# Decode attention on one core: score groups of one key block, a row maximum in halves, and engine programs without a block

## The chip, the cores and the metric

The kernel runs on one core of a Trainium2 chip. A core has five engines that run their own instruction streams and meet at semaphores: TensorE (PE, matmuls and the weight loads ahead of them), VectorE (DVE), ScalarE (ACT), GpSimd (POOL) and SyncE (SP), which here only issues DMAs. The metric is the device time of one execution in microseconds (us). Before the change the median of three executions is 445.27 us (445.12 to 446.51).

## The reference

One decode step of a transformer layer for 8 sequences, one token each:

```
mod = silu(c) @ w_mod                      # 1024 -> six vectors sa, ca, ga, sb, cb, gb
h   = layernorm(x) * (1 + ca) + sa
q   = h @ wq                               # 32 heads of 128
scores = q . k_cache * 128**-0.5           # 4 key/value heads, 8192 keys, each shared by 8 query heads
o   = softmax(scores) @ v_cache
x   = x + ga * (o @ wo)
h   = layernorm(x) * (1 + cb) + sb
x   = x + gb * ((relu(h @ W_gate) * (h @ W_up)) @ W_down)
```

All tensors are bf16. The key and value caches are 8 x 4 x 8192 x 128, 67 MB each; with the weights some 186 MB are read, each byte once.

## The kernel before

The kernel is written as a list of operations (`P.op`), each with its engine, the ranges it reads and the ranges it writes. `Prog` derives the waits from these ranges; each engine runs its own operations in the order in which they stand in the list. There is no scheduler behind it: the list's order is the program's order.

All large inputs come through one ring in SBUF, `arena`, on SP's queue. They are loaded in a fixed order: w_mod in two parts, wq in two, then K and V of each step m = 0 to 15 (4 MB each), wo in two, gate and up in two each, and W_down (wd) in five parts of falling size. `pump` puts the next load into the list as soon as every reader of the range it overwrites stands there; at run time the load waits for that reader. In the loop the ring has room for K and V of two steps, so K of step m+2 is issued when the last transpose of K of step m is done, and V of step m+2 when PV of step m is done.

A step m takes two of the 32 (sequence, key head) pairs, both on the 128 partitions. The keys of a step are eight blocks (`QE` = 2048 bf16 per partition). Its stages:

- `kt_part` (L428, DVE): one block is transposed in 32x32 squares into one of four buffers of `kt`. A block's buffer is free again when the scores that read it are done.
- `qk_part` (L441, PE): the scores of two blocks, i and 4+i, 8 matmuls with 512 columns. There are four stationary operands (`t`, `r`), slices of the padded queries `qpad`; each is used for the first block (h = 0) and at once for the second (h = 1). The scores of h = 0 and h = 1 lie in two neighbouring PSUM banks, and each bank is accumulated over the four groups i.
- `rowmax` (L449, DVE): one maximum over both banks, 1024 wide, negated.
- `spread` (L453, PE) and `headmax` (L458 and L461, DVE): the maximum over the rows that belong to one query.
- `expo` (L467, ACT): the exponential, with the row sums.
- `p_turn` (L474, DVE): P transposed, 64 partitions at a time.
- `pv` (L483, PE): 32 matmuls with V, in two column halves.
- `fold` (L493, L496, DVE) and `fold_pe` (L501, PE): PV's result of step m-1 is gathered; these stand among the operations of step m.

PE's order in a step is: four score groups, spread, fold_pe of the step before, PV. DVE's order is: eight transposes, two folds, row maximum, a fold, headmax, a fold, p_turn. So DVE can turn four blocks of step m+1 while PE runs PV of step m, and then waits until the first score group has freed buffers. `make_qpad` (L421, POOL) writes the queries two steps ahead.

At the end `P.emit` writes each engine's operations into a body of `nc.Block`. Each engine branches from the main block to its body, and leaves it through a barrier of all engines.

Of the kernel before, what the change touches and what calls it, by code (L numbers as in the profile page):

```python
# [7 lines left out]
ALU = mybir.AluOpType  # L8
AX = mybir.AxisListType
# [123 lines left out]
def bass_adaLN_cond__gqa_block_cached__glu_gated_reglu__decode_kernel(nc, A_x, A_k_cache, A_v_cache, A_wq, A_wo, B_x, B_W_gate, B_W_up, B_W_down, c, w_mod, out):  # L133
    B, _, D = A_x.shape
    _, G, Sk, Dh = A_k_cache.shape
# [11 lines left out]
    NKT = 4  # L147
# [4 lines left out]
    P = Prog()  # L152
    with ExitStack() as es:
        E = es.enter_context

        def sb(name, shape, dtype):
            return E(nc.sbuf_tensor(name, shape, dtype))
# [5 lines left out]
        ktb = sb("kt", [128, NKT * 2048], dt.bfloat16)  # L163
# [21 lines left out]
        qpad = sb("qpad", [128, 2, 4, 152], dt.bfloat16)  # L185
        prb = sb("prb", [128, 1024], dt.bfloat16)
        pT = sb("pT", [128, 2, 32, 2, 32], dt.bfloat16)
        negm = sb("negm", [128, 4], dt.float32)
# [14 lines left out]
        ps = E(nc.psum_tensor("ps", [128, 8, 512], dt.float32))  # L203

        sems = {("eng", e): E(nc.semaphore("s_" + e)) for e in P.ENGINES}
# [3 lines left out]
        def R(t, lo=0, hi=1):  # L209
            return (t, lo, hi)  # L210

        def bank(b, n=1):
            return ("ps", b, b + n)

        def slot_r(lo, hi):
            return ("arena", lo, hi)
# [3 lines left out]
        stream, place, cursor = [], {}, [0]  # L220
# [51 lines left out]
        def aff(e, t, base, pat):  # L272
# [7 lines left out]
             reads=[R("identf"), R("rsel")], writes=[R("rsel")])  # L280
# [8 lines left out]
                                     start=True, stop=True), reads=[R("rsel"), R("cx", 0, 2)], writes=[bank(6)])  # L289
# [4 lines left out]
             reads=[R("lt")], writes=[R("lt")])  # L294
        P.op("dve", lambda e: e.reciprocal(lu[:], lt[:]), reads=[R("lt")], writes=[R("lu")])
        P.op("dve", lambda e: e.tensor_tensor(out=hb[:], in0=lu[:], in1=c_r, op=ALU.mult),
             reads=[R("lu"), R("x_r")], writes=[R("hb")])

        def to_T(eng="dve"):
# [5 lines left out]
             reads=[R("identf")], writes=[R("dsel")])  # L305
        P.op("dve", lambda e: e.tensor_reduce(jm[:], identf[:].rearrange("p (g m j) -> p g j m", g=2, j=J), AX.X, ALU.add),
             reads=[R("identf")], writes=[R("jm")])
# [3 lines left out]
             reads=[R("identf")], writes=[R("im")])  # L311
        P.op("dve", lambda e: e.tensor_scalar(out=sel[:].rearrange("p (q r) -> p q r", q=4),
                                              in0=dsel[:, None, :].to_broadcast([128, 4, 32]), scalar1=1.0 / D, scalar2=None,
                                              op0=ALU.mult), reads=[R("dsel")], writes=[R("sel")])
        P.op("dve", lambda e: e.tensor_scalar(out=jms[:], in0=jm[:].rearrange("p g j -> p (g j)"), scalar1=scale, scalar2=None, op0=ALU.mult),
             reads=[R("jm")], writes=[R("jms")])
# [29 lines left out]
        for i in range(2):  # L346
            fns = []
            for kk in range(4 * i, 4 * i + 4):
                w = arena[:, place["wm", i] + (kk % 4) * 6 * D:place["wm", i] + (kk % 4 + 1) * 6 * D].rearrange("p (s j n) -> p s j n", s=6, j=4)
                for pr in range(3):  # L350
                    for j in range(4):
                        fns.append(lambda e, w=w, pr=pr, j=j, kk=kk: e.matmul(  # L352
                            ps[32 * j:32 * j + 32, pr, :], hT[:, kk, :], w[:, 2 * pr:2 * pr + 2, j, :],
                            start=(kk == 0), stop=(kk == KC - 1), tile_position=(0, 32 * j)))
            P.op("pe", fns, reads=[R("hT"), slot_r(place["wm", i], place["wm", i] + 24 * D)], writes=[bank(0, 3)])
        for pr in range(3):
# [3 lines left out]
                 reads=[bank(pr)], writes=[R("mod", 2 * pr, 2 * pr + 2)])  # L360
# [8 lines left out]
        for i in range(2):  # L369
            fns = []  # L370
            for kk in range(4 * i, 4 * i + 4):
                w = arena[:, place["wq", i] + (kk % 4) * 4096:place["wq", i] + (kk % 4 + 1) * 4096].rearrange("p (g z n) -> p g z n", g=4, z=2)
                for z in range(2):
                    for g in range(4):
                        fns.append(lambda e, w=w, z=z, g=g, kk=kk: e.matmul(  # L375
                            ps[32 * g:32 * g + 32, 3 + z, :], hT[:, kk, :], w[:, g, z, :],
                            start=(kk == 0), stop=(kk == KC - 1), tile_position=(0, 32 * g)))
            P.op("pe", fns, reads=[R("hT"), slot_r(place["wq", i], place["wq", i] + 2 * SLOT)], writes=[bank(3, 2)])
        qrep = ktb[:, 0:4096].rearrange("p (u q x) -> p u q x", u=4 * J, q=4)
        for z in range(2):  # L380
# [5 lines left out]
            else:  # L386
# [3 lines left out]
                 reads=[res], writes=[res])  # L390
# [3 lines left out]
        for jh in range(2):  # L394
            fns = []
# [5 lines left out]
            for t in range(2):  # L401
                for r in range(2):
# [3 lines left out]
                    if jh == 0:  # L406
                        P.op("dve", lambda e, s=src, d=dst: e.tensor_copy(d, s), reads=[bank(5 + jh)],
                             writes=[R("qR", u * 2 + jh, u * 2 + jh + 1)])
                    else:
                        P.op("act", lambda e, s=src, d=dst: e.activation(d, s, ACT.Copy), reads=[bank(5 + jh)],  # L410
                             writes=[R("qR", u * 2 + jh, u * 2 + jh + 1)])
# [3 lines left out]
        QE = SLOT // 4  # L415

        def make_qpad(m):
            if m >= M:
                return
            for Q in range(4):  # L420
                P.op("pool", lambda e, n=2 * m + Q // 2, Q=Q: e.tensor_copy(  # L421
                    qpad[32 * Q:32 * Q + 32, m % 2, :, 24 + 32 * Q:32 + 32 * Q], qR[32 * Q:32 * Q + 32, :, n, :]),
                     reads=[R("qR", 0, 8)], writes=[R("qpad", m % 2, m % 2 + 1)])

        def kt_part(m, i, h):
            lo = place["k", m] + (4 * h + i) * QE
            to = (8 * m + 2 * i + h) % NKT * QE
            P.op("dve", lambda e: e.transpose(ktb[:, to:to + QE].bitcast(dt.uint32), arena[:, lo:lo + QE].bitcast(dt.uint32)),  # L428
                 reads=[slot_r(lo, lo + QE)], writes=[R("kt", to, to + QE)])

        def qk_part(m, i):
            fns, rd = [], [R("qpad", m % 2, m % 2 + 1)]
            for h in range(2):
                to = (8 * m + 2 * i + h) % NKT * QE
                rd.append(R("kt", to, to + QE))
            for t in range(2):
                for r in range(2):
                    for h in range(2):
                        to = (8 * m + 2 * i + h) % NKT * QE
                        kv = ktb[:, to:to + QE].rearrange("p (c t k r) -> p c t k r", t=2, k=32, r=2)  # L440
                        fns.append(lambda e, t=t, r=r, h=h, kv=kv: e.matmul(  # L441
                            ps[:, 2 * (m % 2) + h, :].rearrange("p (c k) -> p c k", k=32),
                            qpad[:, m % 2, t * 2 + r, 24 - 8 * i:152 - 8 * i], kv[:, :, t, :, r],
                            start=(i == 0 and t == 0 and r == 0), stop=(i == 3 and t == 1 and r == 1)))
            P.op("pe", fns, reads=rd, writes=[bank(2 * (m % 2), 2)])

        def rowmax(m):
            b = 2 * (m % 2)
            P.op("dve", lambda e: e.tensor_reduce(negm[:, 2:3], ps[:, b:b + 2, :].rearrange("p h n -> p (h n)"), AX.X, ALU.max,  # L449
                                                  negate=True), reads=[bank(b, 2)], writes=[R("negm", 2, 3)])  # L450

        def spread(m):
            P.op("pe", lambda e: e.matmul(ps[:, 4, 0:128], negm[:, 2:3].to_broadcast([128, 128]), identf[:],  # L453
                                         start=True, stop=True), reads=[R("negm", 2, 3), R("identf")], writes=[bank(4)])

# [9 lines left out]
        def expo(m):  # L465
            z = m % 2
            P.op("act", lambda e: e.activation(prb[:], ps[:, 2 * z:2 * z + 2, :].rearrange("p h n -> p (h n)"), ACT.Exp,  # L467
                                               bias=bias[:, z:z + 1], scale=scale, accum_out=lall[:, m:m + 1]),
                 reads=[bank(2 * z, 2), R("bias", z, z + 1)], writes=[R("prb"), R("lall", m, m + 1)])
# [42 lines left out]
        make_qpad(0)  # L512
        make_qpad(1)
        for m in range(M):
            for i in range(4):
                kt_part(m, i, 0)
                kt_part(m, i, 1)
                qk_part(m, i)
            make_qpad(m + 2)
            fold(m - 1, 0)  # L520
            fold(m - 1, 1)
            rowmax(m)
            spread(m)
            fold(m - 1, 2)
            headmax(m)
            expo(m)
            fold(m - 1, 3)
            if m >= 1:
                fold_pe(m - 1)
            if m == M - 1:  # L530
                norm()
            p_turn(m)
            pv(m)
        lr = lx[:].rearrange("p n j -> p (n j)")
        P.op("dve", lambda e: e.reciprocal(lr, ps[:, 7, 0:N * J]), reads=[bank(7)], writes=[R("lx")])
        for i in range(4):
# [5 lines left out]
                                              in0=ps[:, 6, 0:N * J].rearrange("p (b h) -> p h b", b=B),  # L542
                                              in1=lr.rearrange("p (b h) -> p h b", b=B), op=ALU.mult),
             reads=[bank(6), R("lx"), R("oT")], writes=[R("oT")])


        for z in range(2):
            fns = []
            for jj in range(4):
                for g in range(G):  # L550
                    fns.append(lambda e, z=z, jj=jj, g=g: e.matmul(
                        ps[32 * g:32 * g + 32, z, 128 * jj:128 * jj + 128], oT[:, J * g + 4 * z + jj, :], identb[:],
                        start=True, stop=True, tile_position=(0, 32 * g)))
# [4 lines left out]
            else:  # L558
                P.op("act", lambda e, dst=dst, z=z: e.activation(dst, ps[:, z, :], ACT.Copy), reads=[bank(z)],
                     writes=[("kt", 512 * z, 512 * z + 512)])  # L560
        P.op("dve", lambda e: e.transpose(oX, orow.rearrange("p j d -> p (j d)").rearrange("p (x k) -> p k x", k=KO)),  # L561
             reads=[("kt", 0, 1024)], writes=[r_oX])


        for i, (r0, r1) in enumerate(wo_parts):
            lo, hi = place["wo", i], place["wo", i] + (r1 - r0) * D
            w = arena[:, lo:hi].rearrange("p (r j n) -> p r j n", r=r1 - r0, j=4)
            fns = []
            for k in range(r0, r1):
# [6 lines left out]
             reads=[bank(5), R("mod", 2, 3)], writes=[R("lu")])  # L576
        P.op("dve", lambda e: e.tensor_tensor(out=x1[:], in0=lu[:], in1=x_r, op=ALU.add),
             reads=[R("lu"), R("x_r")], writes=[R("x1")])
# [5 lines left out]
        for i, (r0, r1) in enumerate(gu_parts):  # L584
            for nm, b0 in (("gate", 0), ("up", 2)):
                lo, hi = place[nm, i], place[nm, i] + (r1 - r0) * F
                w = arena[:, lo:hi].rearrange("p (r j h n) -> p r j h n", r=r1 - r0, j=4, h=2)
                fns = []
                for kk in range(r0, r1):
                    for h in range(2):  # L590
                        for j in range(4):
                            fns.append(lambda e, w=w, r=kk - r0, kk=kk, h=h, j=j, b0=b0: e.matmul(  # L592
                                ps[32 * j:32 * j + 32, b0 + h, 0:H], hT[:, kk, :], w[:, r, j, h, :],
                                start=(kk == 0), stop=(kk == KC - 1), tile_position=(0, 32 * j)))
                P.op("pe", fns, reads=[R("hT"), slot_r(lo, hi)], writes=[bank(b0, 2)])
        for h in range(2):
            P.op("act", lambda e, h=h: e.activation(grel[:, H * h:H * h + H], ps[:, h, 0:H], ACT.Relu), reads=[bank(h)],
                 writes=[("kt", 4096 + FJ * h, 4096 + FJ * h + FJ)])
            P.op("dve", lambda e, h=h: e.tensor_tensor(out=hrow[:, H * h:H * h + H], in0=ps[:, 2 + h, 0:H],  # L599
                                                       in1=grel[:, H * h:H * h + H], op=ALU.mult),  # L600
                 reads=[bank(2 + h), ("kt", 4096 + FJ * h, 4096 + FJ * h + FJ)], writes=[("kt", 2048 + H * h, 2048 + H * h + H)])
        P.op("dve", lambda e: e.transpose(hmT, hrow.rearrange("p (x k) -> p k x", k=KF)), reads=[("kt", 2048, 2048 + FJ)],
             writes=[r_hmT])
        for i, (r0, r1) in enumerate(wd_parts):
            lo, hi = place["wd", i], place["wd", i] + (r1 - r0) * D
            w = arena[:, lo:hi].rearrange("p (r j n) -> p r j n", r=r1 - r0, j=4)
            fns = []
            for k in range(r0, r1):
# [6 lines left out]
             reads=[bank(4), R("mod", 5, 6)], writes=[R("lu")])  # L615
        P.op("dve", lambda e: e.tensor_tensor(out=ob[:], in0=lu[:], in1=x1[:], op=ALU.add),
             reads=[R("lu"), R("x1")], writes=[R("ob")])
        o2 = out.rearrange("b o d -> (b o) d")
        for j in range(4):
            P.op("sp" if j % 2 == 0 else "act",  # L620
                 lambda e, j=j: e.dma_start(o2[:, 256 * j:256 * (j + 1)], ob[32 * j:32 * j + B, :]),
                 reads=[R("ob")], writes=[("out", j, j + 1)], dma=True)
        P.op("sp", [], reads=[("out", 0, 4)])

        P.plan()
        block = E(nc.Block())
        bass_engs = {"sp": nc.sync, "act": nc.scalar, "pool": nc.gpsimd, "dve": nc.vector, "pe": nc.tensor}
        starters = {"sp": block.sync, "act": block.scalar, "pool": block.gpsimd, "dve": block.vector, "pe": block.tensor}
        for name in P.ENGINES:
            def body(_, name=name):  # L630
                P.emit(name, bass_engs[name], sems)
            starters[name](body)


# [26 lines left out]
```

## Time and profile before

| | before |
|---|---|
| median of 3 executions | 445.27 us |
| the profiled execution, its own time | 446.51 us |
| its span, first to last instruction | 444.7 us |
| mean granted TensorE clock | 0.812 |
| DMA queue of SP | 185.64 MB, 97.7% of 16 engines' span |
| key transposes (L428) | 128 of 1213 ns, 148.0 us |
| score matmuls (L441) | 512, 121.5 us busy |
| PV matmuls (L483) | 512, 91.9 us busy |
| row maximum (L449) | 16 of 1225 ns, 19.6 us |
| spread (L453) | 32 matmul records, 7.8 us |

The profile is of one execution. Busy times of engines overlap, so they don't add up to the span. A matmul's busy time counts from its start to its end through the array, and matmuls follow each other more closely than that. The chain of waits is followed back from the last instruction: what released each piece of work. "us to landing" of a DMA counts from its issue on SP to its completion, the time in the queue included. In a table by stretches of time each row has busy time and number of instructions of PE, PE's weight loads, DVE, ACT and POOL, then the granted clock of TensorE (1.00 is full), the busy share of the DMA engines and GB/s.

### The profile page before, as it was taken

To read this page: it belongs to the slowest core of one execution; us is meant where nothing else is said; L and a number is where in the kernel's file an instruction comes from. 1 tells how busy PE (TensorE), PEld (TensorE's weight loads), DVE (VectorE), ACT (ScalarE), POOL (GpSimd) and SP (SyncE) were. 2 spreads that over 40 slices of the span, in tenths; PEclk is the share of its full clock that TensorE was granted. 3 is DMA by queue.
4 is the path that set the end of the run, shared out by engine and by line. 5 is a ranking of instruction groups with operands and counts; after the bars stand their busy time and mean duration, and the time that the engine had idled before them with its cause. 6 is when DMAs were issued, how large, how long until landed. Compare 5 with 4: busy or idle time off the path is not lost.

```text
span 444.7 us, 3991 instructions
## 1 busy us (share of the span) xinstructions
PE 269.2 (61%) x1691; PEld 121.4 (27%) x1691; DVE 258.9 (58%) x340; ACT 28.8 (6%) x48; POOL 19.8 (4%) x77
## 2 busy tenths in 40 slices
PE   0062427667484949576775849495857668556635
PEld 0021112323132323223232314232322323235312
DVE  0233056667777776857667777767576677753120
ACT  1100011110101010101001010101010010110100
POOL 6000010000000000000000000000000000000000
PEclk9997568696978879696969788797969697876775
DMA  8999999999999999999999999999999999999993
GB/s 354 427 445 426 424 433 454 424 430 426 424 451 433 432 424 427 438 439 430 433 424 427 439 439 429 430 404 424 405 433 385 419 398 406 412 438 424 435 415 158
DMA packets 6946, 185.90 MB, mean 418 GB/s; under 512 B 816, under 2 KB 912, under 8 KB 1168
## 3 DMA queue, kind: packets, MB, share of 16 engines
q1 hardware_dynamic: 6896, 185.64, 97.7%
q8 instruction: 13, 0.21, 0.2%
q14 instruction: 5, 0.04, 0.0%
q10 hardware_dynamic: 32, 0.01, 0.0%
HBM read 185.63 MB, written 0.02 MB: 417 GB/s over the span
## 4 chain that ended last, share of the span: by engine, by line
PE 40%; DVE 35%; DMA 18%; ACT 5%; issue 2%; SPq 0%
PE ps L483 21%; DVE kt L428 17%; PE ps L441 14%; DVE pT L474 9%; DMA arena<-in_w_mod_dram 7%; DMA arena<-in_A_k_cache_dram 6%; DMA arena<-in_B_W_down_dram 5%; DVE negm L449 4%; ACT prb L467 4%; PE ps L453 2%; PE ps L571 1%; DVE mj L458 1%; PE ps L592 1%; DVE mjt L461 1%; PE ps L352 1%
## 5 line engine op out<-in xcount | busy, mean ns | idle before, releaser
L428 DVE STREAM_TRANSPOSE kt<-arena 128x1024 uint32<-128x1024 uint32 x128 | 148.0, 1213 | 52.4 <-PE ps L441 47.6
L441 PE MATMUL ps<-kt,qpad 128*128 128x512 bf16 x512 | 121.5, 383 | 23.2 <-DVE kt L428 23.2
L483 PE MATMUL ps<-arena,pT 128*64 128x512 bf16 x512 | 91.9, 537 | 50.8 <-DVE pT L474 50.8
L441 PEld LDWEIGHTS ps<-kt,qpad 128*128 128x128 bf16 x512 | 45.6, 97 | 97.5 <-DVE kt L428 32.5
L483 PEld LDWEIGHTS ps<-arena,pT 128*64 128x64 bf16 x512 | 43.9, 152 | 93.4 <-issue 87.6
L474 DVE STREAM_TRANSPOSE pT<-prb 64x1024 bf16<-64x1024 bf16 x32 | 39.6, 1239 | 15.9 <-ACT prb L467 15.4
L467 ACT ACTIVATE prb<-ps,bias 128x1024 bf16<-128x1024 f32 x16 | 17.8, 1113 | 290.6 <-DVE mjt L461 290.6
L449 DVE TENSOR_REDUCE negm<-ps 128x1 f32<-128x1024 f32 x16 | 19.6, 1225 | 22.8 <-PE ps L441 22.8
L421 POOL COPY qpad<-qR 32x32 bf16<-32x32 bf16 x64 | 13.0, 203 | 322.5 <-PE ps L441 268.5
L453 PE MATMUL ps<-identf,negm 128*128 128x128 f32 x32 | 7.8, 325 | 21.2 <-DVE negm L449 21.2
L496 DVE SCALAR_TENSOR_TENSOR om<-ps,im,om 128x128 f32<-128x128 f32 x48 | 16.6, 346 | 0.6
L375 PE MATMUL ps<-arena,hT 128*32 128x512 bf16 x64 | 6.8, 602 | 14.1 <-DMA arena<-in_A_wq_dram 14.1
L501 PE MATMUL ps<-jmp,om 128*128 128x16 f32 x32 | 6.3, 272 | 14.7 <-DVE om L496 14.7
L592 PE MATMUL ps<-arena,hT 128*32 128x448 bf16 x128 | 9.3, 464 | 5.9 <-DMA arena<-in_B_W_up_dram 3.5
L453 PEld LDWEIGHTS ps<-identf,negm 128*128 128x128 f32 x32 | 4.7, 186 | 29.1 <-DVE negm L449 27.2
L290 DVE CAST cxr<-ps 128x512 bf16<-128x512 f32 x1 | 0.7, 691 | 19.1 <-PE ps L288 19.1
L288 PE MATMUL ps<-cx,rsel 32*128 32x512 bf16 x1 | 0.6, 582 | 18.5 <-DMA cx<-in_A_x_dram 18.5
L610 PE MATMUL ps<-arena,kt 128*32 128x256 bf16 x112 | 6.9, 415 | 7.5 <-DMA arena<-in_B_W_down_dram 7.5
L385 DVE CAST kt<-ps 128x512 bf16<-128x512 f32 x1 | 0.7, 691 | 17.4 <-PE ps L375 17.4
L501 PEld LDWEIGHTS ps<-jmp,om 128*128 128x128 f32 x32 | 4.8, 188 | 18.0 <-DVE om L496 16.9
L599 DVE TENSOR_TENSOR kt<-ps,kt 128x448 bf16<-128x448 f32 x2 | 1.2, 620 | 13.1 <-PE ps L592 13.1
L571 PE MATMUL ps<-arena,kt 128*32 128x256 bf16 x128 | 6.5, 398 | 2.7 <-DVE kt L561 2.7
(79 smaller groups left out, 93.1 us busy)
## 6 DMA issues: line engine op xcount, KB each, us to landing
arena<-in_A_k_cache_dram SPq DMA_DIRECT2D x16, 4096.0 KB, 22.5
arena<-in_A_v_cache_dram SPq DMA_DIRECT2D x16, 4096.0 KB, 18.1
arena<-in_w_mod_dram SPq DMA_DIRECT2D x2, 6144.0 KB, 17.3
arena<-in_A_wq_dram SPq DMA_DIRECT2D x2, 4096.0 KB, 20.6
arena<-in_A_wo_dram SPq DMA_DIRECT2D x2, 4096.0 KB, 16.0
arena<-in_B_W_gate_dram SPq DMA_DIRECT2D x2, 3584.0 KB, 18.6
arena<-in_B_W_up_dram SPq DMA_DIRECT2D x2, 3584.0 KB, 22.5
arena<-in_B_W_down_dram SPq DMA_DIRECT2D x1, 3584.0 KB, 24.5
```

What stands on the lines that cost most here:

```text
L421: P.op("pool", lambda e, n=2 * m + Q // 2, Q=Q: e.tensor_copy(qpad[32 * Q:32 * Q + 32, m % 2, :, 24 + 32 * Q:32 + 32 * Q], qR[32 * Q:32 * ...
L428: P.op("dve", lambda e: e.transpose(ktb[:, to:to + QE].bitcast(dt.uint32), arena[:, lo:lo + QE].bitcast(dt.uint32)), reads=[slot_r(lo, lo ...
L441: fns.append(lambda e, t=t, r=r, h=h, kv=kv: e.matmul(ps[:, 2 * (m % 2) + h, :].rearrange("p (c k) -> p c k", k=32), qpad[:, m % 2, t * 2 ...
L449: P.op("dve", lambda e: e.tensor_reduce(negm[:, 2:3], ps[:, b:b + 2, :].rearrange("p h n -> p (h n)"), AX.X, ALU.max, negate=True), reads= ...
L453: P.op("pe", lambda e: e.matmul(ps[:, 4, 0:128], negm[:, 2:3].to_broadcast([128, 128]), identf[:], start=True, stop=True), reads=[R("negm" ...
L467: P.op("act", lambda e: e.activation(prb[:], ps[:, 2 * z:2 * z + 2, :].rearrange("p h n -> p (h n)"), ACT.Exp, bias=bias[:, z:z + 1], scal ...
L474: P.op("dve", lambda e, g=g: e.transpose(pT[64 * g:64 * g + 64, z, :, g, :], prb[64 * g:64 * g + 64, :]), reads=[R("prb"), R("pT", z, z + ...
L483: fns.append(lambda e, t=t: e.matmul(ps[64 * (t % 2):64 * (t % 2) + 64, 5, :].rearrange("p (i d) -> p i d", d=Dh), pT[:, z, t].rearrange(" ...
L496: P.op("dve", lambda e, i=i: e.scalar_tensor_tensor(out=om[:], in0=ps[:, 5, Dh * i:Dh * i + Dh], scalar=im[:, i:i + 1], in1=om[:], op0=ALU ...
L501: P.op("pe", lambda e: e.matmul(ps[:, 6, 16 * m:16 * m + 16], om[:], jmp[:].rearrange("p g j -> p (g j)"), start=True, stop=True), reads=[ ...
L571: fns.append(lambda e, w=w, r=k - r0, k=k, j=j: e.matmul(ps[32 * j:32 * j + 32, 5, 0:256], oX[:, k, :], w[:, r, j, :], start=(k == 0), sto ...
L592: fns.append(lambda e, w=w, r=kk - r0, kk=kk, h=h, j=j, b0=b0: e.matmul(ps[32 * j:32 * j + 32, b0 + h, 0:H], hT[:, kk, :], w[:, r, j, h, : ...
```

## The change

There are three edits.

1. Scores. `qk_part` takes one key block in place of two: 4 matmuls a group and eight groups a step, each right behind its own transpose. The blocks are taken in memory order, so groups 0 to 3 fill the first PSUM bank and groups 4 to 7 the second. A stationary operand is used for one matmul and then changed.
2. Row maximum. `rowmax` is called for each bank: 512 wide, for the first bank behind the sixth transpose and score group, for the second where the whole one stood. `spread` begins with the minimum of the two negated values, one element per partition, on DVE.
3. Program. The operations are written into the main block, without `nc.Block`: no branch at the start and no barrier of all engines at the end.

```diff
-        def kt_part(m, i, h):
-            lo = place["k", m] + (4 * h + i) * QE
-            to = (8 * m + 2 * i + h) % NKT * QE
+        def kt_part(m, e8):
+            lo = place["k", m] + e8 * QE
+            to = (8 * m + e8) % NKT * QE
...
-        def qk_part(m, i):
-            fns, rd = [], [R("qpad", m % 2, m % 2 + 1)]
-            for h in range(2):
-                to = (8 * m + 2 * i + h) % NKT * QE
-                rd.append(R("kt", to, to + QE))
+        def qk_part(m, e8):
+            to = (8 * m + e8) % NKT * QE
+            i = e8 % 4
+            b = 2 * (m % 2) + e8 // 4
+            kv = ktb[:, to:to + QE].rearrange("p (c t k r) -> p c t k r", t=2, k=32, r=2)
+            fns = []
             for t in range(2):
                 for r in range(2):
-                    for h in range(2):
...
-        def rowmax(m):
-            b = 2 * (m % 2)
-            P.op("dve", lambda e: e.tensor_reduce(negm[:, 2:3], ps[:, b:b + 2, :].rearrange("p h n -> p (h n)"), AX.X, ALU.max,
-                                                  negate=True), reads=[bank(b, 2)], writes=[R("negm", 2, 3)])
+        def rowmax(m, h):
+            b = 2 * (m % 2) + h
+            P.op("dve", lambda e: e.tensor_reduce(negm[:, h:h + 1], ps[:, b, :], AX.X, ALU.max, negate=True),
+                 reads=[bank(b)], writes=[R("negm", h, h + 1)])
 
         def spread(m):
+            P.op("dve", lambda e: e.tensor_tensor(out=negm[:, 2:3], in0=negm[:, 0:1], in1=negm[:, 1:2], op=ALU.min),
+                 reads=[R("negm", 0, 2)], writes=[R("negm", 2, 3)])
...
-            for i in range(4):
-                kt_part(m, i, 0)
-                kt_part(m, i, 1)
-                qk_part(m, i)
+            for e8 in range(8):
+                kt_part(m, e8)
+                qk_part(m, e8)
+                if e8 == 5:
+                    rowmax(m, 0)
             make_qpad(m + 2)
             fold(m - 1, 0)
             fold(m - 1, 1)
-            rowmax(m)
+            rowmax(m, 1)
             spread(m)
...
-        block = E(nc.Block())
...
-        for name in P.ENGINES:
-            def body(_, name=name):
-                P.emit(name, bass_engs[name], sems)
-            starters[name](body)
+        for name, e in (("sp", nc.sync), ("act", nc.scalar), ("pool", nc.gpsimd), ("dve", nc.vector), ("pe", nc.tensor)):
+            P.emit(name, e, sems)
```

More of the change, by code (lines that the diff above doesn't have):

```diff
@@ L436, in qk_part @@
             for t in range(2):
                 for r in range(2):
-                    for h in range(2):
[L439 to L444, printed above, removed]
@@ L445, in qk_part @@
-            P.op("pe", fns, reads=rd, writes=[bank(2 * (m % 2), 2)])
-        def rowmax(m):
-            b = 2 * (m % 2)
-            P.op("dve", lambda e: e.tensor_reduce(negm[:, 2:3], ps[:, b:b + 2, :].rearrange("p h n -> p (h n)"), AX.X, ALU.max,
-                                                  negate=True), reads=[bank(b, 2)], writes=[R("negm", 2, 3)])
+                    fns.append(lambda e, t=t, r=r: e.matmul(
+                        ps[:, b, :].rearrange("p (c k) -> p c k", k=32), qpad[:, m % 2, t * 2 + r, 24 - 8 * i:152 - 8 * i],
+                        kv[:, :, t, :, r], start=(i == 0 and t == 0 and r == 0), stop=(i == 3 and t == 1 and r == 1)))
@@ L452, in spread @@
+            P.op("pe", fns, reads=[R("kt", to, to + QE), R("qpad", m % 2, m % 2 + 1)], writes=[bank(b)])
+        def rowmax(m, h):
+            b = 2 * (m % 2) + h
+            P.op("dve", lambda e: e.tensor_reduce(negm[:, h:h + 1], ps[:, b, :], AX.X, ALU.max, negate=True),
+                 reads=[bank(b)], writes=[R("negm", h, h + 1)])
         def spread(m):
+            P.op("dve", lambda e: e.tensor_tensor(out=negm[:, 2:3], in0=negm[:, 0:1], in1=negm[:, 1:2], op=ALU.min),
+                 reads=[R("negm", 0, 2)], writes=[R("negm", 2, 3)])
@@ L625, in bass_adaLN_cond__gqa_block_cached__glu_gated_reglu__decode_kernel @@
         P.plan()
-        block = E(nc.Block())
-        bass_engs = {"sp": nc.sync, "act": nc.scalar, "pool": nc.gpsimd, "dve": nc.vector, "pe": nc.tensor}
-        starters = {"sp": block.sync, "act": block.scalar, "pool": block.gpsimd, "dve": block.vector, "pe": block.tensor}
-        for name in P.ENGINES:
-            def body(_, name=name):
-                P.emit(name, bass_engs[name], sems)
-            starters[name](body)
+        for name, e in (("sp", nc.sync), ("act", nc.scalar), ("pool", nc.gpsimd), ("dve", nc.vector), ("pe", nc.tensor)):
+            P.emit(name, e, sems)
 _INS = ['A_x', 'A_k_cache', 'A_v_cache', 'A_wq', 'A_wo', 'B_x', 'B_W_gate', 'B_W_up', 'B_W_down', 'c', 'w_mod']
```

## The prediction

> **What bounds the kernel now.** I read the page first: engine shares, slices, queues.
>
> ```profile
> PE 269.2 (61%) x1691; PEld 121.4 (27%) x1691; DVE 258.9 (58%) x340; ACT 28.8 (6%) x48; POOL 19.8 (4%) x77
> ...
> PEclk9997568696978879696969788797969697876775
> DMA  8999999999999999999999999999999999999993
> GB/s 354 427 445 426 424 433 454 424 430 426 424 451 433 432 424 427 438 439 430 433 424 427 439 439 429 430 404 424 405 433 385 419 398 406 412 438 424 435 415 158
> ...
> q1 hardware_dynamic: 6896, 185.64, 97.7%
> ```
>
> No compute engine is near full, one queue moves everything, and its rate sinks from slice 27 on. Three stretches of the same trace (the last two columns are DMA share and GB/s) price that:
>
> ```profile
> 105.90:305.10 199.20, 136.91 (x666) 59.95 (x662) 139.57 (x176) 12.05 (x20) 8.11 (x40) 0.84 1.00 430
> 305.10:388.60 83.50, 57.26 (x274) 25.06 (x274) 59.67 (x75) 4.82 (x8) 1.62 (x8) 0.83 0.98 411
> 388.60:441.00 52.40, 29.88 (x434) 17.60 (x434) 14.52 (x23) 3.06 (x5) 0.00 (x0) 0.70 0.93 398
> ```
>
> Why it sinks is told by the DMA view, cut to short windows: one V load each, issued at 87.77, 210.86, 313.26 and 374.70 (the last is a wo load of the same size); the last number is us from issue to landing.
>
> ```profile
> arena<-in_A_v_cache_dram SPq DMA_DIRECT2D x1, 4096.0 KB, 23.4
> ...
> arena<-in_A_v_cache_dram SPq DMA_DIRECT2D x1, 4096.0 KB, 16.5
> ...
> arena<-in_A_v_cache_dram SPq DMA_DIRECT2D x1, 4096.0 KB, 13.4
> ...
> arena<-in_A_wo_dram SPq DMA_DIRECT2D x1, 4096.0 KB, 13.9
> ```
>
> 13.1 to 13.4 us is what such a load takes when nothing is queued before it, so the first had some 10.2 us of queue ahead of it, the second 3.3, the third none. The queue lands 4 MB every 9.68 us while it is full (87.77+23.4 = 111.2 to 210.86+16.5 = 227.4 is twelve transfers), 19.36 us for K and V of one step m. The arena holds two steps, and K and V of step m+2 are issued when step m's last key transpose and its PV are done; the issues come every 20.48 us. So compute is 1.12 us a step too slow, the queue drains by that much a step and is dry from about 292 us on. The chain of waits of one step shows what makes 20.48:
>
> ```profile
> 246.06 5.73 PE ps L483 x32
> 251.79 1.85 PE ps L441 x8
> ...
> 253.67 4.63 DVE kt L428 x4
> ...
> 258.35 1.92 PE ps L441 x8
> ...
> 260.29 1.24 DVE negm L449
> ...
> 261.57 0.50 PE ps L453 x2
> ...
> 262.64 1.21 ACT prb L467 x2
> ...
> 263.88 1.25 DVE pT L474
> ...
> 265.15 1.25 DVE pT L474
> ...
> 266.54 0.61 PE ps L483
> ```
>
> It is compute alone, with no DMA in it: PV, a score group, four transposes, a score group, row maximum, spread, exponential, P turned. After the loop the last weights (wd) are waited for again: DMA until 440.4, and 4.3 us of end behind it.
>
> **The scores, four matmuls a group.** The 512 matmuls, 512 weight loads and 128 transposes stay, in number and shape. Start to start is 0.216 us, from the timeline (16 score matmuls in 3.65 us, 8 in 1.92), and the single records show it alike whether the next matmul has the same queries or others; losing the neighbours costs nothing that the trace shows. Four take 1.92 - 4x0.216 = 1.05 us. Count from PV's end (251.79; PE has then started on scores 0.07 earlier). The first group ends at 0.98 in place of 1.86, so transposes 4 and 5 (1.155 each) run to 3.31. The waits of PE on DVE double, from 64 to 128, but these groups wait for blocks that are long turned, except the last two.
>
> **First half of the row maximum.** On DVE it stands behind transpose 5 and ahead of 6 and 7. It needs score group 3, at 3.65-0.07 = 3.58, so DVE stands 0.3 us and transposes 6 and 7 are held. Its duration is not in the trace: the 1024-wide one takes 1225 ns, a 256-wide reduce 420 (L320), which gives 1.05 ns an element and 152 fixed, so 689 for 512. It ends at 4.29, transposes 6 and 7 at 6.62, the last score group at 7.72. PE is not late for it: groups 4 and 5 end near 5.2.
>
> **Second half, and the minimum.** The two folds queued before it (0.31+0.35) fit into the 1.1 us of the last group, as they did. It runs 7.74 to 8.43. The 128x1 minimum has no row; the nearest are 159 and 165 ns (L330, L333), bounds 81 (an accumulator read) and 425 (a 128x256 tensor_tensor). I take 160 and a 30 ns wait, the gap between dependent DVE instructions, so spread starts at 8.66, against 9.78 (261.57) before. That is 1.12 us less a step: 19.36, by chance the queue's own pace. By the bounds of the minimum it is 19.28 to 19.63.
>
> **What the clock makes of it.** PV runs partly at half clock. The granted clock changes in steps of 3.41 us, and 20.48 is six of them:
>
> ```profile
> 243.50:246.91 3.41, 0.85 (x5) 0.44 (x7) 3.34 (x3) 0.00 (x0) 0.00 (x0) 0.50 0.96 413
> 246.91:250.32 3.41, 3.41 (x19) 1.64 (x17) 3.41 (x4) 0.00 (x0) 0.00 (x0) 0.50 1.07 461
> 250.32:253.74 3.42, 3.42 (x24) 1.55 (x21) 0.32 (x2) 0.00 (x0) 0.00 (x0) 1.00 1.06 460
> ...
> 52.35:55.76 3.41, 2.63 (x28) 1.05 (x32) 0.00 (x0) 0.00 (x0) 0.00 (x0) 0.50 0.82 356
> 55.76:59.18 3.42, 1.59 (x44) 0.99 (x36) 2.58 (x7) 0.99 (x4) 0.00 (x0) 1.00 1.06 460
> ```
>
> Before 250.32 a pair of PV matmuls takes 0.43 us, after it half that. A PV that starts 1.12 us earlier and meets the rise at the same step ends only 0.56 earlier; over the steps it slides up to 2.24 us ahead, and if the rise stayed there the period would still be six steps. It need not stay: a 2.24 us slide fills the 243.5 step to (0.85+2.24)/3.41 = 91%, and the lines at 52.35 show the clock rising after one filled to 2.63/3.41 = 77%. So it rises a step sooner now and then and the period is a mixture of five and six steps: walking PV's start on by hand with a 77% threshold gives 19.4, with 90% about 20.0.
>
> The Trainium skill ("TensorE: Matmul & The Clock Gate", Part 1) speaks against the change here: full clock comes after at least one busy window of about 3.4 us "sustained", windows running free. If only a fully busy window counted, the period would stay 20.48 and the sum would be 446.2; the 77% row says less is enough.
>
> **Where the loop's gain stops.** Compute ahead of the queue buys nothing. The 10.2 us of queue at the first V load last for the 14 steps to the last wo load as long as the period is under 19.36+10.2/14 = 20.09. At 19.4 to 20.0 the queue never dries, and the second wo load lands at 111.2+28x9.68 = 382.2 in place of 374.70+13.9 = 388.6: 6.4 us. The 411 against 430 GB/s gives only 83.5x19/430 = 3.7, since a dry spell ends with the engines even again; by the trailing engine 6.4 counts, and I take 6.0. From there on (52.4 us to the end) the queue was full before, and the issues of gate, up and wd come earlier with the loop: nothing gained, at most 1.6 if all ran at 9.68 per 4 MB. What comes after the last weights (final matmuls, two DVE operations, output) is unchanged.
>
> **No block.** Start: the release at 0.66 and SP's first DMA at 0.74, with a branch between: 0 to 0.05. End: SP's last wait is over at 444.35 and the span ends at 444.7, the barrier: 0.2 to 0.35. No loss has a row: the opening barrier stays. I take 0.3.
>
> **Sum.** 6.3 us off the profiled execution's 446.51 (span 444.7 and 1.8 around it): 440.2. That execution is the slowest of the three; from the median 445.27 it is 439.0. The cost bounds: 3.7+0.2 to 6.4+1.6+0.35, so 436.9 to 441.4.
>
> **Rivals.**
> - Half the gain: the period falls to between 20.1 and 20.4, the clock rising late more often than not or the minimum and first half dearer. Each 0.1 us over 20.09 costs 1.4: 441.4 to 444. For it: the path has no spare beyond 0.73 us. Against: the 77% row.
> - No change: the clock keeps the six steps, and only the barrier goes, 445.0. For it: 20.48 held for 14 steps on end.
> - Slower: the change of weights at every matmul shows. Each group of four then grows by x, group 3 ends 4x later and holds the first half row maximum and with it transposes 6 and 7, and the last group adds x: 5x. From x = 1.12/5 = 0.22 us (56 ns a matmul) it decides. With the whole load of 97 ns exposed, x = 0.39, the period is 20.48+0.8 = 21.3 and the queue loses 14x(21.3-19.36)-10.2 = 17 us in place of about 6: 456. Against: 0.216 us at changes of weights that are there already, every second matmul.
>
> **How the numbers follow.** Queue full throughout: 0.81, 439.0, its own range 437 to 441.4. Half the gain: 0.09. No change: 0.06. Slower: 0.04. 0.3% (1.3 us) is what a measurement here can tell from none, so faster 0.90, same 0.06, slower 0.04. The range takes the first case and a part of the second: 436.8 to 442.0.
>
> **What would show it.** K issues every 19.3 to 19.8 us; every V load over 13.4 us from issue to landing; no slice under 420 GB/s between the fifth and the thirty-eighth; last weights landing near 434 to 435; 32 half row maxima of about 0.69 us; five-step as well as six-step distances between rises of the clock. Wrong if K issues still come every 20.48, if score matmuls stand further apart than 0.22, or if the last engine's lag over the others (3 us at the end now) grows, since the end goes by that engine.

## The result and the profile after

The changed kernel takes 439.68 us (median of 6, 439.07 to 440.08) against 445.41 us for the kernel before on the same chip: ratio 0.986, 95% interval 0.984 to 0.988. The forecast was 439.0 us, range 436.8 to 442.0. The profiled execution took 440.03 us, its span went from 444.7 to 438.7 us.

The page of the changed kernel, its busy shares, slices and main queue:

```profile
PE 271.6 (62%) x1691; PEld 121.2 (28%) x1691; DVE 263.6 (60%) x372; ACT 28.8 (7%) x48; POOL 19.8 (5%) x77
...
PEclk9997669697888969698796968888798978685556
DMA  8999999999999999999999999999999999999994
GB/s 359 433 421 444 436 433 429 434 430 429 430 433 430 429 430 430 432 436 434 436 432 433 445 432 430 430 430 432 430 429 428 430 432 437 434 430 430 431 425 180
...
q1 hardware_dynamic: 6896, 185.64, 98.4%
```

The engines do the same work. The sag of the DMA rate from slice 27 on is gone: from the fourth slice to the last but one none is under 425 GB/s. Three stretches that answer to those of before (the last two columns are DMA share and GB/s):

```profile
105.30:303.00 197.70, 144.37 (x694) 63.64 (x693) 151.00 (x203) 12.04 (x20) 8.13 (x40) 0.84 1.00 433
303.00:383.50 80.50, 55.81 (x296) 24.81 (x294) 58.33 (x84) 6.06 (x10) 1.63 (x8) 0.83 1.00 433
383.50:435.40 51.90, 23.97 (x368) 12.73 (x368) 8.44 (x15) 1.82 (x4) 0.00 (x0) 0.60 0.94 404
```

The second stretch had 411 GB/s before. The DMA view in short windows again, for 4 MB loads issued at 85.34, 183.67, 300.19, 338.75 (V) and 358.26 (the second wo load); the last number is us from issue to landing:

```profile
arena<-in_A_v_cache_dram SPq DMA_DIRECT2D x1, 4096.0 KB, 25.7
...
arena<-in_A_v_cache_dram SPq DMA_DIRECT2D x1, 4096.0 KB, 25.1
...
arena<-in_A_v_cache_dram SPq DMA_DIRECT2D x1, 4096.0 KB, 24.7
...
arena<-in_A_v_cache_dram SPq DMA_DIRECT2D x1, 4096.0 KB, 25.5
...
arena<-in_A_wo_dram SPq DMA_DIRECT2D x1, 4096.0 KB, 25.3
```

Before, this number fell from 23.4 to 13.4, which is a load with little or no queue ahead of it (the V loads issued at 292.78 and 354.22 took 12.3 and 14.8). Now it stays. The queue is full from the first step to the last weights. DVE's transposes stood 33.1 us in total for K loads, against 4.3 before, but most of that wait runs beside PV and is not on the chain of waits: behind the first steps the chain of the loop has one K load,

```profile
170.24 28.88 DMA arena<-in_A_k_cache_dram
```

and is compute elsewhere.

One step of the chain of waits, of the changed kernel:

```profile
294.22 5.93 PE ps L482 x32
300.15 3.59 PE ps L439 x16
...
303.77 0.69 DVE negm L446
304.46 2.29 DVE kt L428 x2
...
306.80 1.06 PE ps L439 x4
...
307.88 0.70 DVE negm L446
...
308.60 0.17 DVE negm L450
...
308.81 0.50 PE ps L452 x2
```

From PV's end (300.15) to the spread (308.81) it is 8.66 us, 9.78 before. The order is the one worked out: the first half of the maximum waits for the fourth score group (16 matmuls), two transposes follow it, then the last group of four.

What stands between the two spans, by the landings of the last loads: the second wo load lands at 358.26+25.3 = 383.6, before at 388.6 (5.0 us); from there to the last weights it takes 51.8 in place of 52.4 (0.6); from their landing to the end 3.3 in place of 3.7 (0.4, the barrier). Together 6.0. Another 0.5 us lies outside the span: in the six executions of the changed kernel the time is 1.26 to 1.37 us above the span, in the kernel before it is 1.74 to 1.86 (38 executions of the rounds below; the profiled one, 446.51 - 444.7 = 1.8). So the profiled execution went from 446.51 to 440.03, 6.5 us less.

### The profile page after: what moved, and what is told of

The parts are those of the page before. It is cut to its first block, busy times and chain, and to the rows that moved or that the text cites. A ratio compares the mean times of both kernels' runs of the same rounds, so it can differ in the third digit from the quotient of the medians.

```text
span 438.7 us, 4012 instructions
## 1 busy us (share of the span) xinstructions
PE 271.6 (62%) x1691; PEld 121.2 (28%) x1691; DVE 263.6 (60%) x372; ACT 28.8 (7%) x48; POOL 19.8 (5%) x77
## 4 chain that ended last, share of the span: by engine, by line
PE 35%; DMA 32%; DVE 26%; ACT 4%; issue 2%; SPq 1%
PE ps L482 18%; DMA arena<-in_A_k_cache_dram 15%; PE ps L439 13%; DVE kt L428 10%; DMA arena<-in_A_wq_dram 9%; DMA arena<-in_B_W_down_dram 8%; DVE pT L473 7%; DVE negm L446 4%; ACT prb L466 4%; PE ps L452 1%; PE ps L571 1%; DVE mj L457 1%; PE ps L375 1%; PE ps L592 1%; DVE mjt L460 1%
## 5 line engine op out<-in xcount | busy, mean ns | idle before, releaser
L428 DVE STREAM_TRANSPOSE kt<-arena 128x1024 uint32<-128x1024 uint32 x128 | 149.1, 1215 | 40.4 <-DMA arena<-in_A_k_cache_dram 33.1
L482 PE MATMUL ps<-arena,pT 128*64 128x512 bf16 x512 | 94.0, 547 | 51.1 <-DVE pT L473 51.1
L482 PEld LDWEIGHTS ps<-arena,pT 128*64 128x64 bf16 x512 | 44.8, 155 | 94.5 <-issue 89.7
L446 DVE TENSOR_REDUCE negm<-ps 128x1 f32<-128x512 f32 x32 | 22.1, 689 | 11.7 <-PE ps L439 11.7
L592 PE MATMUL ps<-arena,hT 128*32 128x448 bf16 x128 | 12.7, 577 | 14.5 <-DMA arena<-in_B_W_up_dram 6.8
L610 PE MATMUL ps<-arena,kt 128*32 128x256 bf16 x112 | 6.0, 372 | 9.2 <-DMA arena<-in_B_W_down_dram 9.2
L592 PEld LDWEIGHTS ps<-arena,hT 128*32 128x32 bf16 x128 | 4.5, 139 | 22.0 <-DMA arena<-in_B_W_up_dram 8.4
```

The costliest lines, as they stand in the source:

```text
L446: P.op("dve", lambda e: e.tensor_reduce(negm[:, h:h + 1], ps[:, b, :], AX.X, ALU.max, negate=True), reads=[bank(b)], writes=[R("negm", h, ...
L482: fns.append(lambda e, t=t: e.matmul(ps[64 * (t % 2):64 * (t % 2) + 64, 5, :].rearrange("p (i d) -> p i d", d=Dh), pT[:, z, t].rearrange(" ...
```

## The experiments

Two theories were held against each other. The first: the period of a step counts only where it lets the DMA queue run dry, and the period itself comes in steps of the TensorE clock. The second: the chain's length counts, as it is, either through the queue or with no queue at all. In all experiments "chain" is put on one footing: from PV's end to the next PV's start, plus the 5.73 us that PV takes in the kernel before, where this makes 14.75 + 5.73 = 20.48. It is the period that a step would have if PV always took 5.73 us. "Period" is the measured distance from one PV's start to the next, or from one K issue to the next.

**The whole row maximum back in the changed kernel.**

```diff
-                if e8 == 5:
-                    rowmax(m, 0)
...
-            rowmax(m, 1)
+            rowmax(m)      # 1024 wide, and no minimum in spread
```

> The changed kernel with the row maximum taken whole again, 1024 wide, where the second half stood, and no minimum. Nothing then stands between the transposes: by the working of the prediction the last score group ends 1.0 us sooner and the whole maximum costs 0.55 more, less 0.19 for the minimum, so the chain of a step is some 0.6 us shorter, about 18.7. If the DMA queue is the bound, the shorter chain buys nothing: 439.7, within 0.6. If the gain was the chain itself, another 0.6x15 = 9 us go: 431. If it was the split that gave the gain, 445.

Measured: ratio to the kernel before 0.986 (0.982 to 0.991), the changed kernel's own. What DVE waited for, here and below it in the changed kernel:

```profile
DVE kt L428 <- DMA arena<-in_A_k_cache_dram: 47.3, 16, 4.4
```

```profile
DVE kt L428 <- DMA arena<-in_A_k_cache_dram: 33.1, 16, 3.2
```

A shorter chain turned into 14 us more of waiting for K and no time, and its chain of waits now has a K load in every second step, seven times between 92 and 355 us, as here:

```profile
246.46 29.46 DMA arena<-in_A_k_cache_dram
```

So the queue is the bound here, and the split of the maximum is not what brought the gain. The changed kernel itself stands almost level with the queue: compute alone takes 19.34 us a step (measured below, V loaded once), the queue 2 x 9.73 = 19.46 (from the landings).

**A reduce of 256 on the chain of the changed kernel.**

```diff
+        def linger(m):
+            P.op("dve", lambda e: e.tensor_reduce(negm[:, 3:4], ps[:, 2 * (m % 2), 0:256], AX.X, ALU.max, negate=True),
+                 reads=[bank(2 * (m % 2))], writes=[R("negm", 3, 4)])
...
             rowmax(m, 1)
+            linger(m)
             spread(m)
```

> The changed kernel with one further reduce, 256 wide (0.42 us and a gap), on VectorE between the second half row maximum and the minimum, on the chain of every step; its result goes nowhere. Chain 19.36+0.45 = 19.81. If the queue forgives every period up to 20.09, nothing is lost: 439.7. If the clock holds the period to six of its 3.41 us steps unless PV fills more than about 76% of the step in which it starts, PV slides only 2x(20.48-19.81) = 1.3 us ahead, fills (0.85+1.3)/3.41 = 64%, and every period is 20.48: the whole gain is lost for 0.45 us, 445.

Measured: 439.45 us, ratio 0.985 (0.982 to 0.988): nothing lost. I had expected 445 from the clock, and that was wrong by the size of the addition. The reduce adds 0.21 us to the chain, not 0.45: it starts 0.08 us before the row of the reduce ahead of it ends, and the minimum, which followed its own input after a wait, now stands behind an unrelated operation and has none:

```profile
274.60 0.69 DVE L446 TENSOR_REDUCE negm<-ps 128x1 f32<-128x512 f32 x1 [0.52 <-PE ps L439]
275.21 0.42 DVE L450 TENSOR_REDUCE negm<-ps 128x1 f32<-128x256 f32 x1
275.54 0.15 DVE L454 TENSOR_TENSOR negm<-negm 128x1 f32<-128x1 f32 x1
```

The chain is 19.56, and the period 20.0 on the mean, with PV between 4.9 and 6.6 us. That is under 20.09, so the queue forgives it: the second wo load still takes 17.6 us to land, more than the dry queue's 12.3 to 14.8.

**A reduce of 512 in the same place.**

```diff
-            P.op("dve", lambda e: e.tensor_reduce(negm[:, 3:4], ps[:, 2 * (m % 2), 0:256], AX.X, ALU.max, negate=True),
+            P.op("dve", lambda e: e.tensor_reduce(negm[:, 3:4], ps[:, 2 * (m % 2), :], AX.X, ALU.max, negate=True),
```

> As the changed kernel with the 256-wide reduce, with a 512-wide one. The 256-wide one added 0.21 us to the chain (a reduce starts 0.3 us ahead of the end that its row shows for the one before), so this adds 0.21+256x1.05/1000 = 0.48: chain 19.84. By the clock's steps PV then slides 2x0.64 = 1.3 us ahead, fills (0.85+1.3)/3.41 = 63% of its first step, under the 76% that still did not raise the clock in the changed kernel, so every period is 20.48 with PV at 6.4 us, and the queue runs dry near the end: 443.5 to 445. By the chain's length alone 19.84 is under 20.09: 439.5, as with the 256-wide one.

Measured: 443.37 us, ratio 0.995 (0.993 to 0.998). Chain 19.83 (the overlap between two reduces is 0.08 us, as above, and not the 0.3 of the expectation; the sum of 0.48 held all the same, as it starts from the measured 0.21). From the sixth step on every period but the last is 20.47 to 20.49 with PV at 6.38 us. One step of its chain of waits:

```profile
265.02 6.38 PE ps L486 x32
271.40 3.60 PE ps L439 x16
...
279.12 0.69 DVE negm L446
279.82 0.60 DVE negm L450
280.41 0.08 DVE negm L454
...
285.50 0.61 PE ps L486
```

285.50 - 265.02 = 20.48, with a chain 0.65 us shorter than before: PV takes all of it. A V load issued at 353.36 lands 12.9 us later, the dry queue's number. 0.27 us more on the chain than in the run ahead of it cost 1.0% by the two ratios, 4 to 5 us.

**A reduce of 256 in the kernel before, ahead of its row maximum.**

```diff
+            linger(m)
             rowmax(m)
             spread(m)
```

> The kernel before with the same further reduce, 256 wide, ahead of its row maximum in every step. Chain 20.48+0.45 = 20.93. If the chain's length counts, the queue loses 0.45x14 = 6.3 us more: 451.7. If the clock holds six steps, PV starts later against the rise, has less of it at half clock and gets the 0.45 back: period 20.48 and 445.4, as without it.

Measured: ratio 1.002 (1.000 to 1.005), no loss that can be told. The chain grew by 0.33 us to 20.81; the period stayed 20.48 and PV fell from 5.73 to 5.40 us (one PV and the start of the next):

```profile
246.23 5.40 PE ps L487 x32
...
266.71 0.61 PE ps L487
```

0.33 x 14 = 4.6 us would be 1.0%, outside the interval.

**A reduce of 1024 in the same place.**

```diff
-                                                  ps[:, 2 * (m % 2), 0:256], AX.X, ...
+                                                  ps[:, 2 * (m % 2):2 * (m % 2) + 2, :], AX.X, ...   # both banks
```

> The kernel before with a further reduce of 1024 (1.23 us and a gap) ahead of its row maximum. Chain 21.73. Here PV can't win all of it back in six steps, so both accounts have it slower: by the clock's steps a mixture of six and seven steps, 21.6 on the mean, and 445.4 + 14x(21.6-20.48) = 461; by the chain's length 21.73 and 463; if every us of the chain counted without a queue, 445.4+1.25x16 = 465.

Measured: 461.90 us, ratio 1.036 (1.032 to 1.039). Periods of 20.97, 22.42 and 21.46 in turn, with PV 5.09, 6.53 and 5.57; 21.55 on the mean of the loop. The three accounts lie too close here to be told apart by the time; the pattern is that of the clock's steps.

**Score groups of two blocks in the changed kernel, the split maximum kept.**

```diff
-                qk_part(m, e8)
+                if e8 % 2 == 1:
+                    qk_part(m, e8 // 2)     # 8 matmuls, blocks e8-1 and e8
```

> The changed kernel with score groups of two key blocks again (8 matmuls, blocks in memory order), the row maximum still in halves, no block. Counted from PV's end: first group 1.86, transposes 4 and 5 to 4.19, first half maximum to 4.88, transposes 6 and 7 to 7.2, last group to 9.15, second half and minimum to 10.06: 0.3 us more than before, chain 20.8. By the clock's steps still 20.48 a period and 445, the barrier's 0.3 off; by the chain's length the queue loses 0.3x14 = 4.2 us more than before, 449.5. Either way it shows that the split without the finer groups brings nothing.

Measured: 444.64 us, ratio 0.997 (0.995 to 1.000). Chain 20.74, period 20.48, PV 5.47. The split and the missing block without the finer groups bring about what the missing block brings alone (0.998, next); 449.5 is excluded.

**The block alone.**

```diff
-        block = E(nc.Block())
...
-            starters[name](body)
+        for name, e in (("sp", nc.sync), ("act", nc.scalar), ("pool", nc.gpsimd), ("dve", nc.vector), ("pe", nc.tensor)):
+            P.emit(name, e, sems)
```

> The kernel before, with only the block taken away. Period 20.48 as before; the span ends with SP's last wait and not with a barrier of all engines: 0.3 us less, 445.1, which these rounds can't tell from none; the last lines of the trace can.

Measured: ratio 0.998 (0.994 to 1.001), which by itself settles nothing, as expected. In the trace SP's last wait ends the span; in the kernel before 0.35 us come behind it. And each of its ten executions takes 1.27 to 1.36 us more than its span, where the kernel before takes 1.74 to 1.86. So the block is worth some 0.35 us in the span and 0.5 outside it; the second part was not expected.

**No loads of V, first try.** PV reads the keys in place of the values.

```diff
-            for nm, t in (("k", A_k_cache), ("v", A_v_cache)):
+            for nm, t in (("k", A_k_cache),):
...
-            lo = place["v", m]
+            lo = place["k", m]
```

> The changed kernel without the loads of V: PV reads the keys in place of the values, so that half of the loop's bytes are gone and compute alone sets the period. By the chain's length 19.36 in every step; by the clock's steps a mixture of 18.6, 19.5, 20.0 and 20.3 with PV between 4.9 and 6.6 us, 19.5 to 19.6 on the mean.

Measured: 529.62 us, a failed experiment. `pump` hands a range to the next load when its readers so far are listed, and PV stands in the list behind that point, so PV waited for a later load (102 us in total). Only the last steps, with all loads landed, say something: periods of 18.5, 19.5 and 20.0.

**V loaded once, into a tensor of its own.** Three kernels: before, changed, and changed with the whole maximum. All PVs use step 0's values, and the ring is four slots smaller. The edit, the same in each:

```diff
-    RING = 19 * 4096
+    RING = 15 * 4096
...
+        vfix = sb("vfix", [128, 2 * SLOT], dt.bfloat16)   # one DMA: V of step 0
...
-            for nm, t in (("k", A_k_cache), ("v", A_v_cache)):
+            for nm, t in (("k", A_k_cache),):
...
-            vv = arena[:, lo:lo + 2 * SLOT].rearrange(
+            vv = vfix[:].rearrange(
```

> The kernel before with V loaded once, for step 0, into a tensor of its own that every PV reads, and a ring four slots smaller. The loop then moves 4 MB a step, 9.7 us, and compute alone sets the period. Six steps of the clock: 20.48 in every step, PV 5.73 us, as with the loads.

> The changed kernel with V loaded once. By the chain's length alone 19.36 in every step, all alike; by the clock's steps, with the rise once PV has filled 76 to 77% of a step, a run of periods near 18.6, 19.5, 20.0 and 20.2 that repeats, 19.5 on the mean.

> The changed kernel with the whole row maximum and V loaded once. Chain 18.7. By the chain's length 18.7 in every step; by the clock's steps 18.2 and 19.3 in turn, 18.8 on the mean. If the split helps the chain, it is longer than the changed kernel's, over 19.5.

Measured, one execution each: 465.18, 437.64 and 430.59 us. These times say little, as the 4 MB of V stand ahead of all other loads and the first PV starts 98.2, 89.6 and 90.1 us into the span, against 81.8 in the kernel before; what counts is the period in the loop. DVE waits for a K load once in each, so compute alone sets it: before 20.48 in every step once settled, with PV 5.82; changed 18.54, 19.50, 19.98, again and again, 19.34 on the mean; whole maximum 18.22 and 19.33 in turn, 18.79 on the mean. PV in steps that follow one another (start, duration), in the kernel before, the changed one and the one with the whole maximum:

```profile
262.83 5.82 PE L485 MATMUL ps<-vfix,pT 128*64 128x512 bf16 x32 [3.13 <-DVE pT L477]
```

```profile
244.80 5.00 PE L484 MATMUL ps<-vfix,pT 128*64 128x512 bf16 x32 [3.12 <-DVE pT L476]
263.34 5.96 PE L484 MATMUL ps<-vfix,pT 128*64 128x512 bf16 x32 [3.12 <-DVE pT L476]
282.84 6.45 PE L484 MATMUL ps<-vfix,pT 128*64 128x512 bf16 x32 [3.13 <-DVE pT L476]
```

```profile
240.66 4.97 PE L482 MATMUL ps<-vfix,pT 128*64 128x512 bf16 x32 [3.12 <-DVE pT L474]
...
258.88 6.09 PE L482 MATMUL ps<-vfix,pT 128*64 128x512 bf16 x32 [3.13 <-DVE pT L474]
...
278.21 4.97 PE L482 MATMUL ps<-vfix,pT 128*64 128x512 bf16 x32 [3.13 <-DVE pT L474]
```

In the changed one the rest of the step is the same each time (13.54 us from PV's end to the next start); only PV changes. A chain that counted as it is would have periods all alike. The whole maximum's chain is shorter than the split one's by 0.3 us, not 0.6 as expected: without the hold on the transposes PE is the limit, 32 matmuls of 0.216 us from PV's end.

The runs in one table, sorted by chain (in the runs with V loaded once the stretch from PV's end to the next start is 14.66 us for the kernel before, and their chains are taken against that):

| kernel | chain, us | period, us | time to that of before |
|---|---|---|---|
| changed, whole maximum | 19.06 (with V once) | 18.79 (with V once) | 0.986 |
| changed | 19.36 | 19.57 by K issues | 0.986 |
| changed + 256 | 19.56 | 20.0 | 0.985 |
| changed + 512 | 19.83 | 20.48 | 0.995 |
| before | 20.48 | 20.48 | 1 |
| changed, groups of two blocks | 20.74 | 20.48 | 0.997 |
| before + 256 | 20.81 | 20.48 | 1.002 |
| before + 1024 | 21.62 | 21.55 | 1.036 |

## Why the prediction was right

- **The bound.** That the period of the loop drained the queue was read from issue-to-landing times, and the runs show it from both sides: a shorter chain than the changed kernel's gains nothing, and the period may reach 20.0 at no cost, while at 20.48 the queue is dry near the end. The bound of 20.09 itself is tested no closer than that, and the dry load's 13.1 to 13.4 us, from which its 10.2 us of queue come, is 12.3 to 14.8 over the same trace.
- **The chain.** Spread 8.66 us after PV's end was worked out, 8.66 was measured. The parts hold: last group 1.05 (1.05 to 1.06), half maximum 689 ns (689), minimum 160 (0.16 to 0.17 us). Weight changes at every matmul cost nothing that shows: 16 score matmuls end 3.59 us behind PV's end, 3.58 before (3.65 - 0.07). The rival that needed 56 ns a matmul is out.
- **The clock.** That PV's slide would fill its first clock step far enough to raise the clock sooner held: in the loop the rises lie five or six clock steps apart, where before they lay six apart throughout, and with V loaded once compute alone takes 19.34 us a step, against 19.4 from the walk by hand with a 77% threshold. K issues are 19.57 us apart on the mean (19.3 to 19.8 was named), but with a full queue that is as much the queue's pace (19.46) as compute's. The rival "no change" was nearer than its 0.06 says: 0.48 us more on the chain (the 512-wide reduce) and it is nearly there.
- **The sum.** 6.3 us were forecast for the profiled execution; 6.5 came (6.0 in its span and 0.5 outside), and 5.7 between the medians. The term that was off is the loop's 6.0: it was 5.0, as the second wo load lands at 383.6 and not at 382.2, 9.73 us per 4 MB over the loop in place of 9.68. The trace records 16 landings for each load: the first of them came from 109.21 to 380.39, still 9.68 per 4 MB, and the last fell behind it, from 1.9 us to 3.2 (1.8 and 2.3 at the same two loads before); why was not tried. The last stretch gave 0.6 where nothing was counted (at most 1.6), the barrier 0.4 where 0.3 was taken, and the 1.8 us around the span, taken as fixed, became 1.3. So the loop's term was 1.0 too large and the others together 1.2 too small: that the total came within 0.2 us is partly luck. The last landing of the last weights trailed the median one by 2.4 us (3.1 before), so by that measure this sign of being wrong did not come.
- **What was not foreseen.** Of the three edits the finer groups carry the gain, but for some 0.9 us of the block; they were not run with the block in place, so their share is what the whole maximum (0.986 without the block) leaves after the block's own. The split maximum was counted as a part of the saving (1.12), and a whole maximum with the finer groups would have saved 0.3 more of chain, for no time.

## What to carry to other kernels

Where a queue of loads stays ahead, look at issue-to-landing along the run: if it falls, compute is slower than the transfers even at a DMA share of 98%, and the gain to be had is only what the queue later lacks, not the sum of what the chain saves. A loop whose TensorE part starts cold in every pass may have a period that is a whole number of clock steps; then a small saving can vanish in slower matmuls and a small cost can be free, so test a saving past the edge before calling it useless.

## What the hardware showed that was not expected

The granted clock changes only at a fixed raster of 3.41 us (in each of the 13 traces here every change lies on one raster of 3.413 us, to 2 ns), and a loop with a cold start in each pass can lock to it: chains between 19.83 and 20.81 us all gave a period of 20.48, six clock steps, with PV making up the difference (6.38 to 5.40 us); chains of 19.56 and less, and of 21.62, gave a mixture of periods. The clock as the stretches of the changed kernel show it (first number after DVE, ACT and POOL is the granted clock):

```profile
254.52:257.93 3.41, 2.59 (x14) 1.32 (x16) 1.45 (x2) 0.00 (x0) 0.00 (x0) 0.50 0.96 413
257.93:261.34 3.41, 3.41 (x20) 1.68 (x18) 3.41 (x4) 0.00 (x0) 0.00 (x0) 0.50 1.03 437
...
275.00:278.41 3.41, 2.85 (x14) 1.45 (x16) 2.35 (x3) 0.00 (x0) 0.00 (x0) 0.50 0.98 423
278.41:281.82 3.41, 3.41 (x26) 1.60 (x23) 2.90 (x4) 0.00 (x0) 0.00 (x0) 1.00 1.04 452
```

A clock step filled to 2.59 of 3.41 us (76%) was followed by another at half clock, one filled to 2.85 (83%) by full clock. Over all runs a PV that began 2.61 us before the end of a clock step still missed the rise and one that began 2.62 us before made it, so for PV's matmuls the edge is sharp and lies near 76.5%. It is not the busy share alone that sets it: in the kernel before, other matmuls (448 columns, L592, begun 0.3 us ahead of it) filled a clock step to the same 2.59 us, and full clock followed:

```profile
424.40:427.82 3.42, 2.59 (x32) 0.85 (x20) 0.72 (x2) 0.00 (x0) 0.00 (x0) 0.50 1.07 461
427.82:431.23 3.41, 0.00 (x0) 0.00 (x0) 2.14 (x2) 0.00 (x0) 0.00 (x0) 1.00 0.90 387
```

The Trainium skill ("TensorE: Matmul & The Clock Gate", Part 1) has the raster, 3413 ns and free-running, and asks for at least one busy window; here some three quarters of one were enough. Why the edge lies there was not tried.
